# Sums of k and v and rows of o by head halves of the array, in a fused linear attention and softplus MLP

## The chip, the core and the metric

The kernel runs on one core of a Trainium2 chip. The metric is the device time of one execution in microseconds (us). Engines are named as the profile names them: PE is TensorE (matmul), PEld its weight loads, DVE is VectorE, ACT is ScalarE, POOL is GpSimd, SP is SyncE, which issues the DMA transfers here.

## What is computed

The reference is a linear attention without softmax, normed per head, followed by a two-layer MLP with a softplus between the layers.

```python
# q, k, v: (batch 8, heads 8, seq 576, head_dim 64), f32;  w_in: (512, 2048), w_out: (2048, 512)
kv  = np.einsum('bhsd,bhse->bhde', k, v)          # 64 x 64 per head
o   = np.einsum('bhsd,bhde->bhse', q, kv)
rms = np.sqrt(np.mean(o * o, axis=-1, keepdims=True) + 1e-06)
x   = (o / rms * g_norm)                          # then (B,H,S,D) -> (B*S, H*D) = (4608, 512)
h   = x @ w_in
g   = np.maximum(h, 0.0) + np.log1p(np.exp(-np.abs(h)))
out = g @ w_out
```

## The kernel before

The kernel is written as tasks. Each task names its engine, a planned duration in ns, what it has to wait for, the buffers that it takes and gives back, and a position. A planner in the program simulates the engines with these durations and fixes the order of the instructions on every engine; the chip then runs that order, with semaphores. `P0` is a list of 40 numbers that shift positions: when weights are fetched and converted, and how far ahead of the MLP the attention tiles and their transfers are put.

Tokens are treated in 36 tiles of 128. A batch has 576 tokens, 4.5 tiles, so four of the tiles are split between two batches (`parts(t)` then gives two parts of 64 rows). Three tiles make a block of 384 tokens for the MLP. The MLP, by far the most of the work, splits each f32 operand into three fp32r parts and runs at lines 668 (`h`) and 675 (`s`); the change does not touch it.

PSUM has eight banks: two for `h`, three for the sums `s0` to `s2` of the MLP, one for transposes `tp`, two in the ring `o`:

```python
rings = dict(m=13, xv=2, gv=2, g=2, raw=2, sq=1, ...,
             h=2, o=2, tp=1, s0=1, s1=1, s2=1)
kv_diag = [const.tile([P, NP, P], F32, name=f"kv_diag{i}") for i in range(2)]   # P=128, NP=4 pairs of heads
```

The sums of k and v for a batch. Head h and head h+4 make a pair p. Most batches lay a pair of heads of k side by side, so that one matmul on the whole array gives a 128 x 128 block, of which the two 64 x 64 blocks on the diagonal are wanted. Batches 0 and 1 (`wide_rows`) use a matmul per head, whose output takes half of the partitions:

```python
def kv_of(b):
    wide_rows = b < 2
    bank = slot("o")
    for p in range(NP + 1):                 # four steps of 512 rows in all, then a tail of 64 rows
        ...
            if s is ks and not wide_rows:   # k of batches 2 to 7: two DMAs
                for h in range(2):
                    nc.sync.dma_start(out=x[:, h::2], in_=src[:, h])
            else:
                nc.sync.dma_start(out=x.rearrange("s (h i) d -> s h i d", h=2), in_=src)
        ...
        def run(...):
            kv = new(bank, [P, NP, 2, D]) if p == 0 else bank.tile
            for i in range(4):
                if wide_rows and not tail:
                    for e in range(2):
                        l, r = (x.tile.rearrange("s (h i) d -> s h i d", h=2)[:, e, i] for x in (ks, vs))
                        nc.tensor.matmul(kv[e * D:(e + 1) * D, p, e], lhsT=l, rhs=r, ...)      # L505
                    continue
                if tail:
                    l, r = pairs(ks.tile, i), vs.tile[:, i::NP]
                else:
                    l, r = pairs(ks.tile, i), vs.tile.rearrange("s (h i) d -> s h i d", h=2)[:, :, i]
                nc.tensor.matmul(kv[:, i if tail else p], lhsT=l, rhs=r, ...)                  # L513
        last = add("PE", 1640 if wide_rows and not tail else 820, run, ...)
    kvd = kv_diag[b % 2]
    kv_ready[b] = [                          # the two diagonal blocks; the rest of kv_diag stays zero
        add("ACT", 360, lambda: nc.scalar.copy(kvd[:D, :, :D], bank.tile[:D, :, 0]), ...),
        add("ACT", 360, lambda: nc.scalar.copy(kvd[D:, :, D:], bank.tile[D:, :, 1]), ...)]
```

The rows of o for a tile. q comes transposed as `qT`, a pair of heads on the 128 partitions, and is multiplied by the pair's block-diagonal matrix. After that o is squared and summed (ACT, DVE), the root is taken (POOL), and o is scaled (DVE, `norm`):

```python
def rows(t):
    tp, qT, o, x, r, xp, xg = (slot(n) for n in ("tp", "m", f"s{t}" if t < TB else "o", "x", "r", "tp", "m"))
    def out_rows():
        y = new(o, [P, H, D])
        for b, r0, n, _ in parts(t):
            for p in range(NP):
                nc.tensor.matmul(y[r0:r0 + n, p::NP], lhsT=qT.tile[:, p, r0:r0 + n],           # L530
                                 rhs=kv_diag[b % 2][:, p].rearrange("r (h d) -> r h d", d=D), ...)
    ...
    a = o_task = add("PE", 830 if len(parts(t)) == 1 else 1350, out_rows, turned + need, pos, [o], [qT])
    a = add("ACT", 600, square of o into x, [a], pos, [x])
    a = add("DVE", 690, reduce, [a], pos, [r])
    a = add("POOL", 2300, root, [a], pos)
    a = add("DVE", 700, norm, [a, o_task], pos, [], [o, r])
```

(The line of the square is shortened here to what it does.) Until the MLP's first step, TensorE fills its idle time with matmuls that have no use but to keep it busy (L784).

Of the kernel before, what the change touches and what calls it, by code (L numbers as in the profile page):

```python
# [8 lines left out]
F32 = mybir.dt.float32  # L9
# [3 lines left out]
AF = mybir.ActivationFunctionType  # L13
ALU = mybir.AluOpType
# [4 lines left out]
P = 128  # L19
# [21 lines left out]
class Plan:  # L41
# [101 lines left out]
def kernel(  # L143
# [24 lines left out]
    nc = tc.nc  # L168
    B, H, S, D = q.shape
# [3 lines left out]
    NP = H // 2  # L173
    KD, KF = d_model // P, d_ff // P
    NT = 384
    TB = NT // P
# [6 lines left out]
    PLACES = 8  # L183
    LAST = PHASES[-1]

    P0 = [-71.0, -4.7, -70.3, -8.7, -15.1, -0.5, -23.9, 2.7, -65.0, -28.3, -35.2, -10.7, -25.2, 1.3,
          -0.2, -2.7, 0.5, -17.5, 13.0, 9.5, 5.5, 6.5, -2.0, 2.5, 2.5, 28.0, 15.0, 14.5, 8.5, 44.5,
          49.5, 68.5, 52.5, 72.0, 94.5, 99.5, 115.5, 110.5, 114.5, 8.5]
    CONVERT, FETCH, EARLY, LATER = P0[:8], P0[8:16], P0[16:27], P0[27:]
    BY_PE = 12  # L190
    AT_ONCE = 2 * TB
# [2 lines left out]
    const = ctx.enter_context(tc.tile_pool(name="const", bufs=1))  # L194
    sb = ctx.enter_context(tc.tile_pool(name="sb", bufs=1))
    ps = ctx.enter_context(tc.tile_pool(name="ps", bufs=1, space=PSUM))
    dram = ctx.enter_context(tc.tile_pool(name="dram", bufs=1, space=DRAM))

    ident_r = const.tile([P, P], F32R, name="ident_r")
# [6 lines left out]
    tails = [const.tile([P, H, D], F32, name=f"tail{i}") for i in range(2)]  # L206
    over = const.tile([P, 2 * KF], F32, name="over")
    scale = const.tile([P, 1], F32, name="scale")
    kv_diag = [const.tile([P, NP, P], F32, name=f"kv_diag{i}") for i in range(2)]


    rings = dict(m=13, xv=2, gv=2, g=2, raw=2, sq=1, 
                 tail0=1, tail1=1, qa=1, xb=1, x=2, r=2,
                 h=2, o=2, tp=1, s0=1, s1=1, s2=1)
    rings.update({f"w{i}_{c}": 1 for i in range(2) for c in range(PLACES)})
    PS = {"h", "o", "tp", "s0", "s1", "s2"}
    plan = Plan(rings)
    slot, add = plan.slot, plan.add

    def new(s, shape, dtype=F32):  # L220
        pool = ps if s.ring in PS else sb
        s.tile = pool.tile(shape, dtype, tag=f"{s.ring}_{s.place}", name=f"{s.ring}_{s.place}")
        return s.tile

    def pairs(x, p):

        return x[:, 2 * p:2 * p + 2].rearrange("r h d -> r (h d)")


    def halves(src, e):  # L230

        return src[e * NP:(e + 1) * NP].rearrange("p s d -> s p d")
# [155 lines left out]
    def parts(t):  # L388

        b, s0 = divmod(t * P, S)  # L390
        if s0 + P <= S:
            return [(b, 0, P, s0)]
        return [(b, 0, S - s0, s0), (b + 1, S - s0, P - S + s0, 0)]
# [63 lines left out]
    kv_ready = {}  # L457
    o_tasks = {}

    def x_pos(t):  # L460

        n = t // TB
        return t * EARLY[0] + EARLY[1] if n == 0 else first_step[0, n] - (EARLY[2] if n == 1 else EARLY[3]) + t % TB

    def kv_of(b):

        pos = x_pos(first_tile[b]) - (EARLY[4] if b else EARLY[5])
        wide_rows = b < 2
        bank = slot("o")
        last = None  # L470
        MAIN = 4 * P
        for p in range(NP + 1):
            tail = p == NP
            ks, vs = (slot(f"tail{i}" if tail else "m") for i in range(2))
            n = S - MAIN if tail else P

            def load(src, s, p=p, tail=tail, n=n, ks=ks):
                if tail:
                    s.tile = tails[s is not ks]
                    src = src[b, :, MAIN:]  # L480
                    if s is ks:
                        for e in range(2):
                            nc.sync.dma_start(out=s.tile[:n, e::2], in_=halves(src, e))
                    else:
                        nc.sync.dma_start(out=s.tile[:n], in_=src.rearrange("h s d -> s h d"))
                    return
                x = new(s, [P, H, D])
                src = src[b, p::NP, :MAIN].rearrange("h (s i) d -> s h i d", i=4)
                if s is ks and not wide_rows:
                    for h in range(2):  # L490
                        nc.sync.dma_start(out=x[:, h::2], in_=src[:, h])
                else:
                    nc.sync.dma_start(out=x.rearrange("s (h i) d -> s h i d", h=2), in_=src)

            lds = [add("SP", ns, lambda src=src, s=s, load=load: load(src, s), (), pos - EARLY[6] + 0.5 * p, [s], [],
                       620 if tail else size, behind=int(pos - 2) - 3)
                   for src, s, ns, size in ((k, ks, *((500, 850) if wide_rows and not tail else (900, 1300))), (v, vs, 500, 850))]

            def run(ks=ks, vs=vs, p=p, tail=tail, n=n):
                kv = new(bank, [P, NP, 2, D]) if p == 0 else bank.tile  # L500
                for i in range(4):
                    if wide_rows and not tail:
                        for e in range(2):
                            l, r = (x.tile.rearrange("s (h i) d -> s h i d", h=2)[:, e, i] for x in (ks, vs))
                            nc.tensor.matmul(kv[e * D:(e + 1) * D, p, e], lhsT=l, rhs=r, start=(p == 0 and i == 0),  # L505
                                             stop=False, skip_group_check=True)
                        continue
                    if tail:
                        l, r = pairs(ks.tile, i), vs.tile[:, i::NP]
                    else:  # L510
                        l, r = pairs(ks.tile, i), vs.tile.rearrange("s (h i) d -> s h i d", h=2)[:, :, i]

                    nc.tensor.matmul(kv[:, i if tail else p], lhsT=l, rhs=r, start=(p == 0 and i == 0), stop=tail,  # L513
                                     skip_group_check=True)
            last = add("PE", 1640 if wide_rows and not tail else 820, run, lds + [last], pos + 0.5 * p,
                       [bank] if p == 0 else [], [ks, vs])
        kvd = kv_diag[b % 2]
        old = o_tasks.get(b - 2, [])
        kv_ready[b] = [
            add("ACT", 360, lambda: nc.scalar.copy(kvd[:D, :, :D], bank.tile[:D, :, 0]), [last] + old, pos + 2.5, [], [bank]),  # L520
            add("ACT", 360, lambda: nc.scalar.copy(kvd[D:, :, D:], bank.tile[D:, :, 1]), [last] + old, pos + 2.5, [], [bank])]

    def rows(t):
        pos = x_pos(t)
        tp, qT, o, x, r, xp, xg = (slot(n) for n in ("tp", "m", f"s{t}" if t < TB else "o", "x", "r", "tp", "m"))
        def out_rows():
            y = new(o, [P, H, D])
            for b, r0, n, _ in parts(t):
                for p in range(NP):
                    nc.tensor.matmul(y[r0:r0 + n, p::NP], lhsT=qT.tile[:, p, r0:r0 + n],  # L530
                                     rhs=kv_diag[b % 2][:, p].rearrange("r (h d) -> r h d", d=D),
                                     start=(p == 0), stop=True, skip_group_check=True)

        def reduce():
            nc.vector.tensor_reduce(out=new(r, [P, H]), in_=x.tile, axis=AX.X, op=ALU.add)  # L535
# [3 lines left out]
            nc.gpsimd.tensor_tensor(out=r.tile, in0=r.tile, in1=half, op=ALU.pow)  # L539

        def norm():
            nc.vector.tensor_tensor(out=x.tile, in0=o.tile, in1=r.tile.unsqueeze(2).to_broadcast([P, H, D]), op=ALU.mult)  # L542

        def turn_x():
            y = new(xp, [P, KD, P])
# [8 lines left out]
        turned = []  # L554
        for b, r0, n, s0 in parts(t):
            if b >= 2:
                if b not in q_slots:
# [3 lines left out]
                        out=part_of_qT(n, r0),  # L561
                        in_=q_slots[b].tile.rearrange("k (p s) -> k p s", p=NP)[:, :, s0:s0 + n]),
# [24 lines left out]
            tp = turn_q.__defaults__[-1]  # L587
# [4 lines left out]
            turned.append(add("ACT", 590, lambda n=n, r0=r0, tp=tp: nc.scalar.copy(part_of_qT(n, r0), tp.tile[:, :, :n]),  # L592
                              [a], pos - 1, [qT] if not r0 else [], [tp], follows=turned[-1] if turned else None))
        need = [u for pt in parts(t) for u in kv_ready[pt[0]]]
        a = o_task = add("PE", 830 if len(parts(t)) == 1 else 1350, out_rows, turned + need, pos, [o], [qT])
        for pt in parts(t):
            o_tasks.setdefault(pt[0], []).append(a)
        a = add("ACT", 600, lambda: nc.scalar.activation(new(x, [P, H, D]), o.tile, func=AF.Square,  # L598
                                                              scale=D ** -0.5), [a], pos, [x])
        a = add("DVE", 690, reduce, [a], pos, [r])  # L600
        a = add("POOL", 2300, root, [a], pos)
# [146 lines left out]
        nc.scalar.dma_start(out=g_col[e * D:(e + 1) * D], in_=g_norm.rearrange("(d one) -> d one", one=1))  # L748
    nc.scalar.mul(g_down, g_col, DOWN_G)
    nc.scalar.preload_act_table_set("softplus")  # L750
    scratch = kv_diag[0][:, 0]
    make_identity(nc, scratch)
    nc.vector.tensor_copy(ident_r, scratch)
    nc.scalar.mul(minus_r, ident, -1.0)
    nc.vector.memset(half, -0.5)
    nc.vector.memset(big, 2.0 ** 30)
    for x in kv_diag + tails:
        nc.vector.memset(x, 0.0)

    for c in range(KF):  # L760
# [59 lines left out]
```

## Time and profile before

| | |
|---|---|
| time, median of 3 runs | 917.99 us (917.92 to 919.47) |
| span of the profiled execution | 917.5 us |
| granted TensorE clock | 1.00 |
| HBM read, written | 91.75 MB, 38.80 MB |
| DMA packets | 230,386, of which 127,408 under 512 B |
| k of batches 2 to 7 | 48 issues of 128 KB, median 4.1 us from issue to landing |
| v | 32 issues of 256 KB, median 4.2 us |

The page gives busy time by engine, then the span in 40 slices of about 23 us with the busy share of each in tenths, then the chain of work that ended last, then groups of instructions. A matmul on f32 operands leaves two weight loads and two matmul records. The ends of matmul records are modelled, so that sums of busy time of short groups on PE are longer than what the group occupies; the starts are read better. The attention lies at the beginning: the rows of o run from 23.3 to 319.6 us, the sums of k and v from 9.4 to 271.6 us, and the MLP's first matmul starts at 42.66 us.

### The profile page before, as it was taken

How to read it: one execution, taken by the hardware profiler on the slowest of the kernel's cores; microseconds unless marked ns; L12 is line 12 of the kernel's file. 1: busy time of each engine (PE TensorE's matmuls, PEld its weight loads, DVE VectorE, ACT ScalarE, POOL GpSimd, SP SyncE). 2: the span in 40 equal slices, each digit the busy share in tenths (PEclk: the TensorE clock that was granted, in tenths of full speed). 3: DMA queues.
4: the chain of work that ended last, by engine and by line, in shares of the span. 5: the costliest groups of instructions: out<-in, count | busy, mean ns of one | idle time of the engine just before them, and what ended most of it. 6: DMA issues, size and time to landing. Idle time of an engine off the chain costs nothing.

```text
span 917.5 us, 13377 instructions
## 1 busy us (share of the span) xinstructions
PE 898.1 (98%) x4863; PEld 812.4 (89%) x4863; DVE 626.6 (68%) x1055; ACT 415.1 (45%) x799; POOL 81.2 (9%) x78
## 2 busy tenths in 40 slices
PE   5799999999999999999999999999999999999998
PEld 4689999989998999999999999999999999998987
DVE  5877887875457887789856778888444455555553
ACT  4776555444334656455434455446323333333331
POOL 0324421312122100000000000000000000000000
PEclk9999999999999999999999999999999999999999
DMA  7999999397883654445433434643320433333323
GB/s 226 241 224 224 260 207 203 89 216 147 176 139 108 149 150 127 125 139 172 149 104 127 150 126 139 208 142 122 104 70 33 138 102 103 106 104 104 104 69 104
DMA packets 230386, 131.44 MB, mean 143 GB/s; under 512 B 127408, under 2 KB 204208, under 8 KB 230320
## 3 DMA queue, kind: packets, MB, share of 16 engines
q1 hardware_dynamic: 230160, 130.59, 53.7%
q8 instruction: 38, 0.62, 0.3%
q14 instruction: 28, 0.23, 0.1%
q10 hardware_dynamic: 160, 0.00, 0.0%
HBM read 91.75 MB, written 38.80 MB: 142 GB/s over the span
## 4 chain that ended last, share of the span: by engine, by line
PE 95%; DMA 2%; DVE 1%; ACT 1%; SPq 0%; issue 0%; ACTq 0%
PE s L675 44%; PE h L668 43%; PE o L530 3%; PE o L513 3%; DMA m<-in_v_dram 1%; DMA g_col<-in_g_norm_dram 1%; PE tp L547 0%; DMA tail<-in_k_dram 0%; SPq L608 0%; PE o L505 0%; PE h L367 0%; DVE xv L440 0%; DVE xv L444 0%; PE tp L585 0%; ACT L750 0%
## 5 line engine op out<-in xcount | busy, mean ns | idle before, releaser
L668 PE MATMUL h<-xv,w 128*128 128x384 f32 x2304 | 434.3, 337 | 0.9 <-ACT g L688 0.9
L675 PE MATMUL s<-w,gv 128*128 128x512 f32 x1728 | 434.2, 395 | 0.0
L668 PEld LDWEIGHTS h<-xv,w 128*128 128x128 f32 x2304 | 406.6, 188 | 15.9 <-ACT g L688 1.1
L675 PEld LDWEIGHTS s<-w,gv 128*128 128x128 f32 x1728 | 319.4, 188 | 58.9 <-issue 0.5
L688 ACT ACTIVATE g<-h 128x384 f32<-128x384 f32 x192 | 94.3, 491 | 392.7 <-PE h L668 388.2
L679 DVE TENSOR_TENSOR gv<-g,gv 128x384 fp32r<-128x384 f32 x192 | 106.4, 554 | 179.1 <-ACT gv L690 178.2
L690 ACT ACTIVATE gv<-g 128x384 fp32r<-128x384 f32 x192 | 100.9, 525 | 22.9 <-PE s L675 15.6
L683 DVE SCALAR_TENSOR_TENSOR gv<-gv 128x384 fp32r<-128x384 f32 x192 | 106.9, 557 | 6.1
L440 DVE SCALAR_TENSOR_TENSOR xv<-m,g_col,xv 128x512 fp32r<-128x512 f32 x102 | 75.9, 744 | 1.3 <-ACT xv L437 1.1
L444 DVE SCALAR_TENSOR_TENSOR xv<-xv 128x512 fp32r<-128x512 f32 x108 | 74.4, 689 | 2.6
L437 ACT ACTIVATE xv<-m,g_down 128x512 fp32r<-128x512 f32 x102 | 69.5, 710 | 1.1 <-DMA m<-x 1.1
L539 POOL TENSOR_TENSOR r<-r,half 128x8 f32<-128x8 f32 x36 | 65.5, 1818 | 3.0
L715 DVE SCALAR_TENSOR_TENSOR m<-s,scale,m 128x512 f32<-128x512 f32 x24 | 17.9, 747 | 30.1 <-PE s L675 30.1
L530 PE MATMUL o<-kv_diag,m 128*128 128x128 f32 (+1 forms) x296 | 36.9, 275 | 0.0
L530 PEld LDWEIGHTS o<-kv_diag,m 128*128 128x128 f32 (+1 forms) x296 | 35.1, 179 | 2.0 <-issue 1.0
L538 POOL TENSOR_SCALAR r<-r 128x8 f32<-128x8 f32 x36 | 15.1, 419 | 240.9 <-DVE r L535 240.6
L715 DVE SCALAR_TENSOR_TENSOR m<-s,m 128x512 f32<-128x512 f32 x36 | 23.7, 684 | 13.5 <-PE s L675 13.4
L542 DVE TENSOR_TENSOR x<-o,r 128x512 f32<-128x512 f32 x33 | 22.7, 687 | 13.5 <-POOL r L539 13.4
L535 DVE TENSOR_REDUCE r<-x 128x8 f32<-128x512 f32 x36 | 24.5, 680 | 10.2 <-ACT x L598 10.0
L303 ACT ACTIVATE sq<-sq,big 128x512 bf16<-128x512 bf16 x32 | 22.9, 717 | 11.2 <-DVE m L299 11.1
L286 ACT ACTIVATE sq<-raw 128x512 bf16<-128x512 bf16 x32 | 21.2, 664 | 12.5 <-DMA raw<-in_moe_w_in_dram 8.3
L299 DVE SCALAR_TENSOR_TENSOR m<-sq,m 128x512 f32<-128x512 bf16 x32 | 22.1, 690 | 6.3 <-ACT sq L286 4.9
(69 smaller groups left out, 452.8 us busy)
## 6 DMA issues: line engine op xcount, KB each, us to landing
m<-x SPq DMA_DIRECT2D x102, 256.0 KB, 4.7
part<-m SPq DMA_DIRECT2D x72, 256.0 KB, 2.7
m<-part SPq DMA_DIRECT2D x72, 256.0 KB, 3.7
raw<-in_moe_w_in_dram SPq DMA_DIRECT2D x16, 512.0 KB, 5.7
m<-in_v_dram SPq DMA_DIRECT2D x32, 256.0 KB, 4.2
raw<-in_moe_w_out_dram SPq DMA_DIRECT2D x16, 512.0 KB, 5.1
qa<-in_q_dram SPq DMA_DIRECT2D x24, 288.0 KB, 6.3
m<-in_k_dram SPq DMA_DIRECT2D x48, 128.0 KB, 4.1
```

Of the source, the lines that this page charges most:

```text
L437: nc.scalar.activation(cols(0, F32R), x.tile, func=AF.Identity, scale=g_down)
L440: nc.vector.scalar_tensor_tensor(out=cols(1, F32R), in0=x.tile, scalar=g_col, in1=cols(0), op0=ALU.mult, op1=ALU.subtract)
L444: nc.vector.scalar_tensor_tensor(out=cols(2, F32R), in0=cols(1), scalar=-RADIX, in1=cols(0), op0=ALU.mult, op1=ALU.add)
L530: nc.tensor.matmul(y[r0:r0 + n, p::NP], lhsT=qT.tile[:, p, r0:r0 + n], rhs=kv_diag[b % 2][:, p].rearrange("r (h d) -> r h d", d=D), start= ...
L539: nc.gpsimd.tensor_tensor(out=r.tile, in0=r.tile, in1=half, op=ALU.pow)
L668: nc.tensor.matmul(hp, lhsT=w_in.tile[:, i, kd * P:(kd + 1) * P], rhs=xv.tile[:, i, kd], start=(m == 0), stop=(m == 3 * KD - 1))
L675: nc.tensor.matmul(mine[i].tile, lhsT=gv.tile[:, m, i * P:(i + 1) * P], rhs=w_out.tile[:, m], start=(c == cs[0] and m == 0), stop=(c == cs ...
L679: nc.vector.tensor_tensor(out=gv.tile[:, 1], in0=g.tile, in1=gv.tile.bitcast(F32)[:, 0], op=ALU.subtract)
L683: nc.vector.scalar_tensor_tensor(out=gv.tile[:, 2], in0=f32[:, 1], scalar=-RADIX, in1=f32[:, 0], op0=ALU.mult, op1=ALU.add)
L688: a = add("ACT", 490, lambda: nc.scalar.activation(new(g, [P, NT]), h.tile, func=AF.Softplus, scale=1.0 + E), [a], s, [g], [h])
L690: a = add("ACT", 530, lambda: nc.scalar.activation(new(gv, [P, 3, NT], F32R)[:, 0], g.tile, func=AF.Copy, scale=DOWN), [a], s, [gv])
L715: a = add("DVE", 700, lambda: nc.vector.scalar_tensor_tensor(out=new(ot, [P, d_model]), in0=bank.tile, scalar=(scale if ph == LAST else 1. ...
```

## The change

The sums of k and v are formed a head at a time for all batches: the head's 64 columns of k are the weights, and its output takes one half of the partitions, so two heads use the two column halves of the array. The block-diagonal matrix goes away; `kv` holds for each pair one head in the upper and one in the lower 64 partitions, and is copied out in one instruction. The rows of o are also formed a head at a time: a head's 64 rows of qT and its 64 x 64 matrix use one row half of the array. The outputs of the two row halves go to two different banks. A tile's o is then half of each of two banks, and the two places of the ring `o` are the two halves of the same pair of banks. The sums of k and v no longer use `o`: batches 0 and 1 use `s0` and `s1`, the others `tp`. All of k is loaded in one DMA per step, in runs of four rows of a head (1 KB), as v is. The planned durations and the positions `P0` are set anew. The aim is to let the two halves of the array work at the same time on f32 matmuls that before computed zeros, or blocks that nobody needs.

```diff
-    P0 = [-71.0, -4.7, -70.3, -8.7, -15.1, -0.5, -23.9, 2.7, -65.0, -28.3, -35.2, ...]
+    P0 = [-76.5, -1.2, -72.8, -8.7, -7.1, 2.0, -30.9, 0.7, -53.5, -44.8, -49.2, ...]
+    o_banks = ps.tile([P, 2, 2, NP, D], F32, name="o_banks")
-    kv_diag = [const.tile([P, NP, P], F32, name=f"kv_diag{i}") for i in range(2)]
+    kvs = [const.tile([P, NP, D], F32, name=f"kv{i}") for i in range(2)]
-    PS = {"h", "o", "tp", "s0", "s1", "s2"}
+    PS = {"h", "tp", "s0", "s1", "s2"}
 ... kv_of
-        wide_rows = b < 2
-        bank = slot("o")
+        bank = slot(f"s{b}" if b < 2 else "tp")
 ...
-                if s is ks and not wide_rows:
-                    for h in range(2):
-                        nc.sync.dma_start(out=x[:, h::2], in_=src[:, h])
-                else:
-                    nc.sync.dma_start(out=x.rearrange("s (h i) d -> s h i d", h=2), in_=src)
+                nc.sync.dma_start(out=new(s, [P, 2, 4, D]), in_=src[b, p::NP, :MAIN].rearrange("h (s i) d -> s h i d", i=4))
 ...
+                    for e in range(2):
+                        l, r = (x.tile[:, i + e * NP] if tail else x.tile[:, e, i] for x in (ks, vs))
+                        nc.tensor.matmul(kv[e * D:(e + 1) * D, i if tail else p], lhsT=l, rhs=r,
+                                         start=(p == 0 and i == 0), stop=tail, skip_group_check=True)
-            last = add("PE", 1640 if wide_rows and not tail else 820, run, ...)
+            last = add("PE", 450, run, lds + [last], pos + 0.5 * p, [bank] if p == 0 else [], [ks, vs])
+        kv_ready[b] = [add("ACT", 400, lambda: nc.scalar.copy(kvs[b % 2], bank.tile), ...)]
 ... rows
-        tp, qT, o, x, r, xp, xg = (slot(n) for n in ("tp", "m", f"s{t}" if t < TB else "o", "x", "r", "tp", "m"))
+        tp, qT, o, x, r, xp, xg = (slot(n) for n in ("tp", "m", "o", "x", "r", "tp", "m"))
 ...
-                    nc.tensor.matmul(y[r0:r0 + n, p::NP], lhsT=qT.tile[:, p, r0:r0 + n],
-                                     rhs=kv_diag[b % 2][:, p].rearrange("r (h d) -> r h d", d=D),
-                                     start=(p == 0), stop=True, skip_group_check=True)
+                    for e in range(2):
+                        nc.tensor.matmul(o_of()[r0:r0 + n, e, p], lhsT=qT.tile[e * D:(e + 1) * D, p, r0:r0 + n],
+                                         rhs=kvs[b % 2][e * D:(e + 1) * D, p], start=True, stop=True)
+        def o_of():
+            return o_banks[:, :, o.place]
 ...
-        a = o_task = add("PE", 830 if len(parts(t)) == 1 else 1350, out_rows, turned + need, pos, [o], [qT])
+        a = o_task = add("PE", 500, out_rows, turned + need, pos, [o], [qT])
 ... at the start: one tile fewer kind to clear
-    for x in kv_diag + tails:
+    for x in tails:
         nc.vector.memset(x, 0.0)
```

More of the change, by code (lines that the diff above doesn't have):

```diff
@@ L184 @@
     LAST = PHASES[-1]
-    P0 = [-71.0, -4.7, -70.3, -8.7, -15.1, -0.5, -23.9, 2.7, -65.0, -28.3, -35.2, -10.7, -25.2, 1.3,
-          -0.2, -2.7, 0.5, -17.5, 13.0, 9.5, 5.5, 6.5, -2.0, 2.5, 2.5, 28.0, 15.0, 14.5, 8.5, 44.5,
-          49.5, 68.5, 52.5, 72.0, 94.5, 99.5, 115.5, 110.5, 114.5, 8.5]
+    P0 = [-76.5, -1.2, -72.8, -8.7, -7.1, 2.0, -30.9, 0.7, -53.5, -44.8, -49.2, -10.7, -28.2, 0.8, -0.2,
+          -3.7, 0.5, -17.0, 13.0, 9.5, 5.5, 6.0, -2.0, 2.5, 3.5, 32.5, -5.5, 14.5, 8.5, 41.5, 47.5,
+          68.0, 54.5, 73.5, 89.5, 95.5, 115.5, 110.5, 114.0, 8.5]
     CONVERT, FETCH, EARLY, LATER = P0[:8], P0[8:16], P0[16:27], P0[27:]
@@ L479, in load @@
                     s.tile = tails[s is not ks]
[L480 to L483, printed above, removed]
-                    else:
-                        nc.sync.dma_start(out=s.tile[:n], in_=src.rearrange("h s d -> s h d"))
-                    return
-                x = new(s, [P, H, D])
-                src = src[b, p::NP, :MAIN].rearrange("h (s i) d -> s h i d", i=4)
@@ L489, in load @@
-                if s is ks and not wide_rows:
-                    for h in range(2):
-                        nc.sync.dma_start(out=x[:, h::2], in_=src[:, h])
-                else:
-                    nc.sync.dma_start(out=x.rearrange("s (h i) d -> s h i d", h=2), in_=src)
-            lds = [add("SP", ns, lambda src=src, s=s, load=load: load(src, s), (), pos - EARLY[6] + 0.5 * p, [s], [],
-                       620 if tail else size, behind=int(pos - 2) - 3)
-                   for src, s, ns, size in ((k, ks, *((500, 850) if wide_rows and not tail else (900, 1300))), (v, vs, 500, 850))]
@@ L499, in run @@
-            def run(ks=ks, vs=vs, p=p, tail=tail, n=n):
-                kv = new(bank, [P, NP, 2, D]) if p == 0 else bank.tile
-                for i in range(4):
[L502 to L521, printed above, removed]
+                    nc.sync.dma_start(out=s.tile[:n], in_=src[b, :, MAIN:].rearrange("h s d -> s h d"))
@@ new lines, in load, with run @@
+                    return
+                nc.sync.dma_start(out=new(s, [P, 2, 4, D]), in_=src[b, p::NP, :MAIN].rearrange("h (s i) d -> s h i d", i=4))
+            lds = [add("SP", 500, lambda src=src, s=s, load=load: load(src, s), (), pos - EARLY[6] + 0.5 * p, [s], [],
+                       650 if tail else 850, behind=int(pos - 2) - 3) for src, s in ((k, ks), (v, vs))]
+            def run(ks=ks, vs=vs, p=p, tail=tail):
+                kv = new(bank, [P, NP, D]) if p == 0 else bank.tile
+                for i in range(4):
+                    for e in range(2):
+                        l, r = (x.tile[:, i + e * NP] if tail else x.tile[:, e, i] for x in (ks, vs))
+                        nc.tensor.matmul(kv[e * D:(e + 1) * D, i if tail else p], lhsT=l, rhs=r,
+                                         start=(p == 0 and i == 0), stop=tail, skip_group_check=True)
@@ L523, in rows, with heads @@
+            last = add("PE", 450, run, lds + [last], pos + 0.5 * p, [bank] if p == 0 else [], [ks, vs])
+        kv_ready[b] = [add("ACT", 400, lambda: nc.scalar.copy(kvs[b % 2], bank.tile), [last] + o_tasks.get(b - 2, []),
+                           pos + 2.5, [], [bank])]
+    def heads(x):
+        return x.rearrange("s (e p) d -> s e p d", e=2)
     def rows(t):
         pos = x_pos(t)
-        tp, qT, o, x, r, xp, xg = (slot(n) for n in ("tp", "m", f"s{t}" if t < TB else "o", "x", "r", "tp", "m"))
+        tp, qT, o, x, r, xp, xg = (slot(n) for n in ("tp", "m", "o", "x", "r", "tp", "m"))
@@ L526, in out_rows @@
         def out_rows():
-            y = new(o, [P, H, D])
             for b, r0, n, _ in parts(t):
                 for p in range(NP):
-                    nc.tensor.matmul(y[r0:r0 + n, p::NP], lhsT=qT.tile[:, p, r0:r0 + n],
-                                     rhs=kv_diag[b % 2][:, p].rearrange("r (h d) -> r h d", d=D),
-                                     start=(p == 0), stop=True, skip_group_check=True)
+                    for e in range(2):
+                        nc.tensor.matmul(o_of()[r0:r0 + n, e, p], lhsT=qT.tile[e * D:(e + 1) * D, p, r0:r0 + n],
+                                         rhs=kvs[b % 2][e * D:(e + 1) * D, p], start=True, stop=True)
@@ L541, in norm @@
         def norm():
-            nc.vector.tensor_tensor(out=x.tile, in0=o.tile, in1=r.tile.unsqueeze(2).to_broadcast([P, H, D]), op=ALU.mult)
+            nc.vector.tensor_tensor(out=heads(x.tile), in0=o_of(), in1=r.tile.rearrange("s (e p) -> s e p", e=2).unsqueeze(
+                3).to_broadcast([P, 2, NP, D]), op=ALU.mult)
         def turn_x():
@@ L594, in rows @@
         need = [u for pt in parts(t) for u in kv_ready[pt[0]]]
-        a = o_task = add("PE", 830 if len(parts(t)) == 1 else 1350, out_rows, turned + need, pos, [o], [qT])
+        a = o_task = add("PE", 500, out_rows, turned + need, pos, [o], [qT])
         for pt in parts(t):
             o_tasks.setdefault(pt[0], []).append(a)
-        a = add("ACT", 600, lambda: nc.scalar.activation(new(x, [P, H, D]), o.tile, func=AF.Square,
+        a = add("ACT", 600, lambda: nc.scalar.activation(heads(new(x, [P, H, D])), o_of(), func=AF.Square,
                                                               scale=D ** -0.5), [a], pos, [x])
@@ L750 @@
     nc.scalar.preload_act_table_set("softplus")
-    scratch = kv_diag[0][:, 0]
+    scratch = kvs[0].rearrange("r p d -> r (p d)")[:, :P]
     make_identity(nc, scratch)
```

## The prediction

> **What bounds the kernel now.** I read the busy shares and slices of the page first, then the chain, the groups by shape, and last the order of single instructions on TensorE.
>
> ```profile
> PE 898.1 (98%) x4863; PEld 812.4 (89%) x4863; DVE 626.6 (68%) x1055; ACT 415.1 (45%) x799; POOL 81.2 (9%) x78
> ...
> PE   5799999999999999999999999999999999999998
> PEclk9999999999999999999999999999999999999999
> DMA  7999999397883654445433434643320433333323
> ...
> PE s L675 44%; PE h L668 43%; PE o L530 3%; PE o L513 3%; DMA m<-in_v_dram 1%; DMA g_col<-in_g_norm_dram 1%; PE tp L547 0%; DMA tail<-in_k_dram 0%; SPq L608 0%; PE o L505 0%; PE h L367 0%; DVE xv L440 0%; DVE xv L444 0%; PE tp L585 0%; ACT L750 0%
> ```
>
> From the third slice (46 us) to the end TensorE has no hole, at full clock, and the chain is 95% PE. So an instruction taken off TensorE after about 40 us shortens the run by what it occupied, until something else becomes the bound. Before 40 us it does not: by the windows PE is busy 26.8 of those 40 us, 7.4 of them with the filler matmuls of L784, while the DMA share is 0.86.
>
> The change touches the sums of k and v (L505, L513) and the rows of o (L530). By shape:
>
> ```profile
> L530 PE MATMUL o<-kv_diag,m 128*128 128x128 f32 x232 | 30.5, 274 | 0.0
> L513 PE MATMUL o<-m,m 128*128 128x128 f32 x192 | 24.9, 275 | 0.7 <-DMA m<-in_v_dram 0.7
> ...
> L513 PE MATMUL o<-tail,tail 128*128 128x128 f32 x64 | 8.9, 283 | 0.0
> ...
> L505 PE MATMUL o<-m,m 128*64 128x64 f32 x128 | 7.0, 272 | 6.8 <-DMA m<-in_v_dram 6.8
> ...
> L530 PE MATMUL o<-kv_diag,m 128*64 128x128 f32 x64 | 6.3, 279 | 0.0
> ```
>
> One matmul call on f32 leaves two records (96 calls of L513 with m are x192), so four calls, one group, are 8 records. The busy sums contain modelled ends (8 records read 1.05 us), so I take starts from the order of time:
>
> ```profile
> 65.00 0.97 PEld L530 LDWEIGHTS o<-kv_diag,m 128*128 128x128 f32 x8
> 65.11 1.06 PE L530 MATMUL o<-kv_diag,m 128*128 128x128 f32 x8
> ...
> 65.90 0.19 PEld L366 LDWEIGHTS h<-w,ident_r 128*128 128x128 f32 x1
> ```
>
> The weight loads of the group begin at 65.00 and those of the next task at 65.90: a full-array group occupies **0.90 us**, and the single records start 112 ns apart. The same holds for L513. This is the unit that must shrink.
>
> The kernel before already has one piece in the new form: the sums of batches 0 and 1 at L505, one head on each column half.
>
> ```profile
> 30.64 0.69 PE L505 MATMUL o<-m,m 128*64 128x64 f32 x16 [1.40 <-DMA m<-in_v_dram]
> 31.26 0.66 PE L547 MATMUL tp<-ident_r,x 128*128 128x128 f32 x4
> ```
>
> Here 16 records start between 30.64 and 31.10, 29 to 31 ns apart on average, though each half streams its own record in about 58 ns: two halves at once. They occupy 0.47 us; the next task starts 0.15 us after the last record.
>
> **What the Trainium skill says.** (1) TensorE: Matmul & The Clock Gate, section LDWEIGHTS (loading the stationary operand): a load takes its columns over 1.2 per ns, whatever the number of rows. The trace agrees: loads of 128 columns read 192 ns and of 64 columns 138 ns, 54 ns for 64 columns; and around L741, whose matmul has one column only, successive 128-column loads start 108 ns apart (632.915, 633.023). (2) TensorEngine Tiling (Array Packing), Key Properties: different tiles can load and multiply in parallel, and changing the tiling drains the engine. L505 shows the first for column halves. For the second: from an L675 matmul to a half-array one takes 0.327 us against 0.231 to the next L675 one; from L668 0.268 against 0.174; out of the split rows of L530 0.202 against 0.109. Each switch costs **0.095 us**. (3) Same page, Gotcha 1: PSUM Pressure: row tiles may not write one bank at the same time. That is why the two halves of o get two banks; no run here shows it yet. (4) PSUM — Partial Sum Buffer, PSUM bank collisions raise a hardware error: two engines may not be in one bank and quadrant at once. In the change both places of o lie in the same two banks, so accesses to one place must be kept apart from those to the other. The trace before, with a bank per place, cannot show what that costs.
>
> **Part 1: sums of k and v.** By the windows 16 of L513's 256 records come before 40 us, so 240 records, 30 groups, lie on the saturated engine. Each goes from 0.90 to 0.47 us of records plus at most two switches, 0.47 + 0.19 = 0.66: 0.24 saved when alone, 0.33 where a neighbour uses the same tiling and a switch falls away. At 0.27 this is 30 x 0.27 = **8 us saved**. L505 itself keeps its form.
>
> **Part 2: rows of o.** 36 tiles, four of them split between two batches. 32 of 320 records come before 40 us; after it are 28 full groups and all 4 split tiles. Now lhsT has 64 rows and still 128 columns, against 64 moving columns. The matmul part of a record halves to some 54 ns, but its weight load is still 128 columns, about 110 ns. Everything hangs on what row halves do with their loads:
> - A: the loads cost no more than in L505. A group is 0.47 + 0.19 = 0.66, saving 0.24; 28 x 0.24 = 6.7 us.
> - B: the two halves load in parallel but each needs its 110 ns: 8 x 0.112 + 0.19 = 1.09, a loss of 0.19; 28 x 0.19 = 5.3 us lost.
> - C: the loads queue: 16 x 0.107 + 0.19 = 1.90, a loss of 1.0; 28 us lost.
>
> Split tiles now occupy 1.51 us and a switch in, 1.60. Afterwards loads and streams both have 64 columns: 32 records at 29 ns plus 0.19 = 1.12, saving 0.5 x 4 = 2 us in each case.
>
> **Part 3: transfers.** For batches 2 to 7 k comes now as two 128 KB issues in 256-byte runs: 6 x 8 x 512 = 24,576 runs become 6,144, 18,432 fewer of 230,160 packets of the queue (8%). PE waited for a v transfer after 40 us only 0.7 us in all, so this is headroom: the windows give a DMA share of 1.00 and 1.06 at 40 to 120 us, where a shorter TensorE schedule would otherwise run into DMA. Together with the re-tuned positions and two memsets fewer at the start I allow 2.5 us gained, a guess.
>
> **Part 4: copies and banks.** Two ACT copies of 64 partitions (353 ns each) become one of about 400; ACT is not the bound. The kv sums move to the s banks and to tp, which has one place. The shared banks of o order the square and the norm of one tile against the rows of the next; the norm is some 4 us behind its rows (square 0.6, reduce 0.68, POOL 2.2, norm 0.69), and 36 tiles pass in about 290 us, so mostly they miss each other. I allow 1 us of new PE waits.
>
> **Sums.** A: -8 - 6.7 - 2 - 2.5 + 1 = -18, 900 us. B: -8 + 5.3 - 2 - 2.5 + 1 = -6, **912 us**. C: -8 + 28 - 2 - 2.5 + 1 = +16, 934 us.
>
> **The rivals.** Case B is what the two load figures say, as the number of rows does not shorten a load. For A speaks the change itself: its plan books 500 ns for a group of rows (830 before) and 450 for a group of sums (820 before), and the earlier bookings match the trace within a tenth (0.90, and 0.43 for transposes booked at 440). Somebody may have measured 500. Against it: 500 is also booked for split tiles, booked at 1350 before, so it may be no measurement. C contradicts the page on tiling and would have made the booking wrong by a factor of four. A further rival: PE waits at the shared banks of o or at tp, several us when square or norm runs late, with DVE busy 78 to 82% in 40 to 160 us. It would add 5 to 10 us to any case. Last, DMA could hold the shortened stretch at 40 to 120 us and take back some of part 1; the wider runs of k speak against that.
>
> **Range and chances.** I give A 0.32, B 0.60, C 0.08. The weighted mean is 0.32 x 900 + 0.60 x 912 + 0.08 x 934 = 910; as the plan's positions have been tuned again for this form, I set 908. Faster by over 2% means under 899.6: half of A and a little of B, 0.22. Slower by over 2% means over 936.4: half of C and a little for waits, 0.05. Range 894 to 922, from a good A to a B with waits.
>
> **What would show it.** Right for part 1: the sums all have 128*64 records, 16 in a group, starts 29 to 31 ns apart, 0.095 us more at both ends. For part 2 the spacing of the 64*128 records of the rows decides: about 30 ns on average is A, 55 is B, 107 is C. Waits of PE on ACT or DVE by name of o_banks or tp, or idle PE slices between 40 and 320 us, would show the bank rival. Packets should fall by about 18,000. I am wrong if the rows are spaced as in A and the time still stays above 905, or if the gain comes from before 40 us, where I book almost nothing.

## Result and profile after

The changed kernel takes 924.93 us (median of 4 runs, 923.5 to 927.33) against 918.03 us (917.92 to 919.47): a ratio of 1.0074, 95% interval 1.005 to 1.0099. It is slower by 6.9 us; the prediction had a gain of 10.

The page of the changed kernel, in the order of the lines shown before:

```profile
PE 907.5 (98%) x5457; PEld 802.3 (87%) x5457; DVE 624.4 (68%) x1053; ACT 413.3 (45%) x791; POOL 79.5 (9%) x78
...
PE   7989999999999999999999999999999999999998
...
DMA packets 211447, 131.52 MB, mean 143 GB/s; under 512 B 102320, under 2 KB 185264, under 8 KB 211376
...
PE s L660 44%; PE h L653 43%; PE o_banks L512 4%; PE tp L495 2%; DMA g_col<-in_g_norm_dram 1%; PE tp L532 1%; PE h L769 0%; PE tp L570 0%; DMA m<-in_q_dram 0%; DVE r L519 0%; DVE xv L441 0%; DVE x L526 0%; POOL r L523 0%; ACT m L592 0%; PE s L495 0%
```

PE still ends the run. The chain is 4% rows and 2% sums where it was 3% and 3%; and the third slice, about 46 to 69 us, shows an 8 where the kernel before has a 9. Packets fell by 18,939; 18,432 had been worked out.

The groups by shape on PE (line, tile of the array, shape and count, then busy us and mean ns):

```profile
L512 PE MATMUL o_banks<-kv,m 64*128 64x64 f32 x512 | 35.5, 278 | 0.4 <-DVE x L526 0.3
L769 PE MATMUL h<-ident_r 128*128 128x512 f32 x39 | 17.4, 554 | 1.7 <-DVE ident_r L738 1.6
L495 PE MATMUL tp<-m,m 128*64 128x64 f32 x384 | 16.0, 228 | 0.0
...
L512 PE MATMUL o_banks<-kv,m 64*64 64x64 f32 x128 | 3.9, 224 | 0.3 <-DVE x L526 0.3
```

The last line is the four split tiles. Filler (L769) rose from 21 matmuls to 39. In order of time, groups of rows and of sums in the kernel before (the view ends inside the last group):

```profile
86.44 1.06 PE L530 MATMUL o<-kv_diag,m 128*128 128x128 f32 x8
87.26 0.94 PE L675 MATMUL s<-w,gv 128*128 128x512 f32 x3
88.04 1.05 PE L513 MATMUL o<-m,m 128*128 128x128 f32 x8
88.85 0.94 PE L675 MATMUL s<-w,gv 128*128 128x512 f32 x3
89.63 0.61 PE L513 MATMUL o<-tail,tail 128*128 128x128 f32 x4
```

and in the changed kernel:

```profile
88.67 1.11 PE L512 MATMUL o_banks<-kv,m 64*128 64x64 f32 x16
89.71 1.65 PE L660 MATMUL s<-w,gv 128*128 128x512 f32 x6
91.30 0.69 PE L495 MATMUL tp<-m,m 128*64 128x64 f32 x16
91.91 0.96 PE L660 MATMUL s<-w,gv 128*128 128x512 f32 x3
92.80 0.69 PE L495 MATMUL tp<-tail,tail 128*64 128x64 f32 x16
```

From the start of a rows group to the next task are 1.04 us, from that of a sums group 0.61. Over all neighbours of one kind, records of rows (64*128) start 55.8 ns apart on average, records of sums (128*64) 32.5 ns, and records of the split tiles (64*64) 24 ns. So the sums are spaced about as L505 had shown, and the rows as in case B.

The cost of a whole group is another matter. A sums group and the three `s` matmuls behind it take 1.50 us (91.30 to 92.80) where they took 1.59 (88.04 to 89.63): 0.09 us saved, and not 0.24 to 0.33. A rows group and six `s` matmuls take 2.63 us (88.67 to 91.30); without three of them, at 0.231 each, that is 1.94, against 1.60 before (86.44 to 88.04): 0.34 lost, and not 0.19. The single starts around the sums group at 91.30 show where it goes: 0.09 us more than usual before the first record, 0.46 from the first record to the last, 0.15 from there to the next task, and 0.10 more than usual between that task's first two matmuls, about 0.8 in all. Groups that stand alone between MLP matmuls take 0.80 to 0.82 us for sums and 1.23 us or more for rows, against 0.89 on the whole array.

Case B gave 912 us by the prediction's sum, not 925. The group cost is one part of what is missing. A new hole is another. The stretch behind the sums of batch 2, all engines:

```profile
57.03 0.69 PE L495 MATMUL tp<-m,m 128*64 128x64 f32 x16
...
62.06 0.64 PE L495 MATMUL tp<-tail,tail 128*64 128x64 f32 x16
...
62.74 0.37 ACT L498 COPY kv<-tp 128x256 f32<-128x256 f32 x1 [2.18 <-PE tp L495]
...
63.17 0.66 PE L532 MATMUL tp<-ident_r,x 128*128 128x128 f32 x4 [0.47 <-ACT kv L498]
...
63.86 0.69 ACT L438 ACTIVATE xv<-tp,g_down 128x512 fp32r<-128x512 f32 x1 [0.21 <-PE tp L532]
...
65.06 0.75 DVE L441 SCALAR_TENSOR_TENSOR xv<-tp,g_col,xv 128x512 fp32r<-128x512 f32 x1 [0.69 <-ACT m L592]
...
65.87 1.12 PE L570 MATMUL tp<-ident_r,m 128*128 128x128 f32 x4 [2.04 <-DVE xv L441]
...
66.64 0.78 PE L367 MATMUL h<-w,ident_r 128*128 128x512 f32 x1
```

The sums of batch 2 hold the bank tp from 57.03 us to the end of their copy at 63.1. Transposes that need tp line up behind them, and each must be read out by ACT and DVE before the next may write: PE waits 0.47 us, then 2.04 us. After the hole the matmuls run slowly (a group of four transposes 1.12 us instead of 0.60 to 0.66); the windows give a granted clock of 0.66 over these 5 us, and of 0.50 from 66 to 68 us (columns: stretch, busy us of PE, PEld, DVE, ACT, POOL, then PEclk):

```profile
65.00:70.00 5.00, 4.13 (x27) 3.19 (x28) 3.81 (x6) 2.47 (x6) 0.00 (x0) 0.66 0.85 132
```

Also the first MLP matmul starts at 43.97 us instead of 42.66.

### The profile page after: what moved, and what is told of

It is laid out like the page before. It is cut to its first block, busy times and chain, and to the rows that moved or that the text cites. A ratio compares the mean times of both kernels' runs of the same rounds, so it can differ in the third digit from the quotient of the medians.

```text
span 922.5 us, 14514 instructions
## 1 busy us (share of the span) xinstructions
PE 907.5 (98%) x5457; PEld 802.3 (87%) x5457; DVE 624.4 (68%) x1053; ACT 413.3 (45%) x791; POOL 79.5 (9%) x78
## 4 chain that ended last, share of the span: by engine, by line
PE 95%; DVE 2%; ACT 1%; DMA 1%; issue 0%; POOL 0%; ACTq 0%; SPq 0%; DVEq 0%
PE s L660 44%; PE h L653 43%; PE o_banks L512 4%; PE tp L495 2%; DMA g_col<-in_g_norm_dram 1%; PE tp L532 1%; PE h L769 0%; PE tp L570 0%; DMA m<-in_q_dram 0%; DVE r L519 0%; DVE xv L441 0%; DVE x L526 0%; POOL r L523 0%; ACT m L592 0%; PE s L495 0%
## 5 line engine op out<-in xcount | busy, mean ns | idle before, releaser
L523 POOL TENSOR_TENSOR r<-r,half 128x8 f32<-128x8 f32 x36 | 63.2, 1755 | 3.0
L512 PEld LDWEIGHTS o_banks<-kv,m 64*128 64x128 f32 (+1 forms) x640 | 34.4, 176 | 10.0 <-issue 6.4
L512 PE MATMUL o_banks<-kv,m 64*128 64x64 f32 (+1 forms) x640 | 39.3, 267 | 0.8 <-DVE x L526 0.7
L526 DVE TENSOR_TENSOR x<-o_banks,r 128x512 f32<-128x512 f32 x36 | 24.7, 686 | 20.2 <-PE o_banks L512 9.8
L583 ACT ACTIVATE x<-o_banks 128x512 f32<-128x512 f32 x36 | 21.4, 599 | 21.2 <-PE o_banks L512 17.1
L352 DVE TENSOR_TENSOR m<-m,w 128x512 f32<-128x512 f32 x30 | 20.5, 685 | 9.5 <-ACT w L349 9.5
```

The costliest lines, as they stand in the source:

```text
L512: nc.tensor.matmul(o_of()[r0:r0 + n, e, p], lhsT=qT.tile[e * D:(e + 1) * D, p, r0:r0 + n], rhs=kvs[b % 2][e * D:(e + 1) * D, p], start=Tru ...
```

## Experiments

Each was timed in five rounds beside the kernel before, which read 917.9 to 918.4 us. A run's ratio and interval are against that kernel. The median of the changed kernel is itself known to about 2.3 us either way, so differences to it of 1 or 2 us are not clear of noise.

**1. Sums in halves, alone, in the old order.** From the kernel before:

```diff
-                if s is ks and not wide_rows:        # k in two DMAs
+                if s is ks and not halves_too:       # halves_too = True
-                    if wide_rows and not tail:
+                    if halves_too and not tail:
```

> The kernel before, in which all batches form their sums a head at a time on column halves and load k in 1 KB runs; tails and rows stay on the whole array, and the planned durations, so the order of instructions, stay untouched. Theory one (the halves of the sums pay, those of the rows do not): 24 groups after 43 us shrink by 0.18 to 0.24 us each, 4.3 to 5.8 us, so 912 to 914. Theory two (the switches of tiling eat the gain of the sums too): 917 to 919. Theory three (the loss lies in the new order alone): the sums gain here as theory one says, so this run parts two from the others.

Measured: 916.06 us, ratio 0.9977 (0.997 to 0.9984). A gain, but of 1.9 us and not 4 to 6: theory two, the cost of the switches, has most of the truth. At 0.09 us a group, as read above, the 24 groups give about 2.

**2. Rows back on the whole array, in the order of the change** (block-diagonal matrix, two copies by ACT, one bank a place, planned durations untouched):

```diff
-   nc.tensor.matmul(o_of()[r0:r0 + n, e, p], lhsT=qT.tile[e * D:(e + 1) * D, p, r0:r0 + n], rhs=kvs[b % 2][e * D:(e + 1) * D, p], ...)
+   nc.tensor.matmul(y[r0:r0 + n, p::NP], lhsT=qT.tile[:, p, r0:r0 + n], rhs=kv_diag[b % 2][:, p]..., ...)
```

> The changed kernel with its order of instructions untouched, but with the rows of o back on the whole array (a pair at a time with the block-diagonal matrix, a bank for each place of o). Theory one: each of some 28 whole groups becomes 0.13 us shorter, the four split tiles some 0.4 us longer, so 2 to 3 us less than the changed kernel, 922 to 923. Theory three (order alone): no difference beyond 1 us, 924 to 926. Were the shared banks of o a cost on TensorE, it would fall by more than 4 us.

Measured: 919.78 us, ratio 1.0017 (1.0008 to 1.0026), 5.1 us under the changed kernel. The row halves cost more than the expectation had. The sign set for the shared banks, over 4 us, was passed, but in the changed kernel's trace PE waits only 0.7 us in all on o_banks.

**3. Sums back on the whole array, in the order of the change**, with k in two transfers and two copies by ACT:

```diff
-                    for e in range(2):   # kv[e * D:(e + 1) * D, ...], a head at a time
+                    nc.tensor.matmul(kv[:, i if tail else p], lhsT=pairs(...), rhs=..., ...)
```

> The changed kernel with its order of instructions untouched, but with the sums as before (whole array but for the steps of batches 0 and 1, k in two transfers of 256-byte runs); the rows stay on row halves. Theory one: 30 groups become 0.2 us longer, 930 to 932. Theory two (sums in halves do not pay): 924 to 926 or less. Theory three: 930 to 932 as well, for the sums are then innocent.

Measured: 930.89 us, ratio 1.0142 (1.0128 to 1.0156): 6.0 us worse, as theories one and three had it. The sums in halves, with their loads of k, are worth 6 us in this order; part of that is a longer spell of half clock, 68.7 to 75.6 us against 65.3 to 68.7 in the changed kernel.

**4. The changed kernel with the old positions**, `P0` alone put back.

> The changed kernel with the list of positions P0 of the kernel before, nothing else. Theory three (the loss lies in the new order): 915 to 919. Theory one with the instructions to blame: within 2 us of the changed kernel, 923 to 927. If transposes still wait at the single bank of tp while the sums of batch 2 sit in it, PE idle of 2 to 3 us near 60 us stays as it is.

Measured: 930.01 us, ratio 1.013 (1.0117 to 1.0144). Both expectations missed: the new positions save the changed kernel 5.1 us. They are not its fault. The idle of 2.3 us at tp is there with the old ones too.

**5. All sums in halves, tails too, in the old order** (as 1, with `if halves_too:` and the tail of k in one DMA).

> As the earlier run with sums in halves in the order of the kernel before, and now the tails too (all 40 groups of the sums on column halves, all of k in its natural layout); rows on the whole array, order untouched. Theory one: 6 more groups after 43 us at 0.15 to 0.24 us, and six pairs of switches that fall away where a tail follows a step: 1 to 2 us under 916.1, so 914 to 915. If the tails gain nothing: 916.

Measured: 915.13 us, ratio 0.9963 (0.9951 to 0.9976). The lowest of all (12 and 18 are level with it), and it beats both kernels. The sums of batch 2 in this trace sit in a bank of o, and the transposes in tp run between them, without a wait:

```profile
57.85 0.69 PE L503 MATMUL o<-m,m 128*64 128x64 f32 x16
58.47 0.66 PE L583 MATMUL tp<-ident_r,m 128*128 128x128 f32 x4
59.05 0.69 PE L503 MATMUL o<-m,m 128*64 128x64 f32 x16
59.80 0.66 PE L583 MATMUL tp<-ident_r,m 128*128 128x128 f32 x4
60.39 0.69 PE L503 MATMUL o<-tail,tail 128*64 128x64 f32 x16
```

**6. Rows in 64 x 64 tiles**: the changed kernel with twice as many row matmuls, of 64 tokens each, which shortens the weight loads to 64 columns and uses four tiles of the array in place of two.

```diff
-            for b, r0, n, _ in parts(t):
+            for b, r0, n in [(b, r, 64) for b, r0, n, _ in parts(t) for r in range(r0, r0 + n, 64)]:
```

> The changed kernel, order untouched, in which each row matmul of 128 tokens is cut into two of 64 tokens: twice as many instructions, 64 x 64 tiles, weight loads of 64 columns. Theory one (rows are bound by the 128-column loads): a group becomes 32 records at 24 to 28 ns instead of 16 at 56, 0.1 us shorter, 28 whole groups: 2 to 4 us less, 921 to 923. If the streaming of the 64 moving columns or the count of instructions bounds the rows instead, the time rises by up to 0.9 us a group, to 940 or more.

Measured: 921.06 us, ratio 1.0033 (1.002 to 1.0045), 3.9 us less. The group with twice the instructions is the shorter one:

```profile
54.10 0.97 PE L512 MATMUL o_banks<-kv,m 64*64 64x64 f32 x32
55.01 2.37 PE L660 MATMUL s<-w,gv 128*128 128x512 f32 x9
```

0.91 us for 32 records against 1.04 for 16. The moving side is 64 columns in both, so neither streaming nor the count of instructions bounds the rows. In the changed kernel each row half starts a record every 112 ns, near the 108 ns at which 128-column loads follow each other at L741: the loads are the likely bound. The run does not part shorter loads from four tiles working at once.

**7. As 2, with the sums in the ring o** (`bank = slot("o")`); the planner finds another order.

> The changed kernel with rows on the whole array, as run before at 919.8, but the sums of k and v accumulate in the ring o, as in the kernel before, and no longer in tp and s. Its planner finds another order, the positions P0 are those of the change. Theory four (the single bank of tp, shared by sums and transposes, costs 3 to 4 us near 62 to 68 us): 915 to 917 and no idle stretch of PE over 1 us after 45 us. If tp is innocent: 919 to 921.

Measured: 920.94 us, ratio 1.0029 (1.0019 to 1.0039). That is the number of an innocent tp. The hole at 62 to 68 us is gone, but a wait at tp of 0.8 us, before 61.5 us, and others elsewhere have come, for instance 1.0 us before 185.86 for ACT, and the MLP starts at 45.58 us. So taking the sums out of tp does not by itself win the loss back.

**8. The kernel before with the new positions.**

> The kernel before with the list of positions P0 of the change, nothing else. If the new positions were good in themselves it would be at or under 918; if they are fitted to the other form, as the old ones proved to be for the changed kernel (5 us), 920 to 925.

Measured: 918.56 us, ratio 1.0003 (0.9994 to 1.0011): neutral, between the two expectations.

**9. Transposes of tiles 5 to 7 in h**, out of the way of the sums in tp:

```diff
-        tp, qT, o, x, r, xp, xg = (slot(n) for n in ("tp", "m", "o", "x", "r", "tp", "m"))
+        tp, qT, o, x, r, xp, xg = (slot(n) for n in ("tp", "m", "o", "x", "r", "h" if 5 <= t < 8 else "tp", "m"))
```

> The changed kernel, in which the transposes of x of tiles 5 to 7 go to a bank of h instead of tp; up to the sums of batch 2 the order on TensorE stays. Theory four (tp is held by the sums of batch 2 and the transposes pile up behind it): the idle 2 us at 64 to 66 us and the slow matmuls after it go, the MLP is 3 to 4 us further at 80 us, and the time is 921 to 922. If the tp stall only moves or h becomes the stall instead: 924 to 926.

Measured: 923.32 us, ratio 1.0054 (1.0042 to 1.0066), 1.6 us less than the changed kernel, between the two expectations and not clear of noise. No wait over 0.5 us is left between 43 and 90 us, and from the first MLP matmul to 15 us of MLP work (matmuls of `h` and `s` at 174 and 231 ns) it takes 30.4 us against 33.4. But its MLP started at 45.69 us, with the same order on TensorE up to there as the changed kernel's 43.97: that start varies between executions. The clock was at half for 10.2 us of this start (9.9 to 13.3 and 16.7 to 23.5 us), and for 3.4 us of the other (17.5 to 20.9).

**10. Less filler**: the filler booked at 700 ns in the changed kernel, 20 of them instead of 39.

> The changed kernel with the filler matmul booked at 700 ns instead of 400, so that the planner inserts fewer of them before the MLP. Theory five (the shorter bookings of the sums made room for 18 more fillers, which take longer than booked and delay the start): the first MLP matmul at 42.5 to 43 us instead of 44.0, the time 1 to 1.5 us less, 923.4 to 924. If the filler is innocent: 924 to 926, or more where the clock drops.

Measured: 926.66 us (923.55 to 929.22), ratio 1.0085 (1.0068 to 1.0102). In the profiled execution the MLP starts at 42.90 us as theory five had it, the hole at tp stays (longest wait 2.0 us), and the median gains nothing.

**11. As 5, all sums booked at 500 ns** instead of 1640 and 820, k booked like v.

> All sums in halves in the kernel before (915.1 with the old bookings), now booked at 500 ns a group, near what they take, and the loads of k as those of v. Theory six (bookings near the truth give a better order): 912 to 914. Theory five (short bookings bring filler and a later start): the first MLP matmul 1 to 3 us later and 916 to 918.

Measured: 918.47 us, ratio 0.9999 (0.999 to 1.0008), 3.3 us worse than 5, with 36 fillers and a first MLP matmul at 45.01 us. Between 43 and 100 us PE idles 2.6 us against 0.1 in 5, most of it a wait of 1.6 us for a copy of the sums.

**12. As 5, with the new positions.**

> All sums in halves in the kernel before, old bookings, with the list P0 of the change. P0 alone moved the kernel before by 0.6 us at most. If it is neutral here too: 914.5 to 916.5; if it suits halves in general: 912 to 914.

Measured: 915.48 us, ratio 0.9967 (0.9954 to 0.998): neutral again. Its MLP starts at 44.75 us, 2 us later than in 5, so a late start by itself is not a loss.

**13. The changed kernel with only the first sums booked long:**

```diff
-            last = add("PE", 450, run, ...)
+            last = add("PE", (1640 if not tail else 820) if b < 2 else 450, run, ...)
```

> The changed kernel, in which only the sums of batches 0 and 1 are booked as long as before (1640 ns a step, 820 the tail), so that the planner leaves the start as dense in filler as before or less. Theory five b (the short bookings at the start, not the filler's own, delay the MLP and let the clock fall): the first MLP matmul at 42.5 to 43.5 us with a clock of 1.0 in the first slices, and 2 to 3 us less than the changed kernel, 922 to 923. If bookings at the start are innocent: 924 to 927.

Measured: 926.81 us, ratio 1.009 (1.0077 to 1.0103). The MLP starts at 41.92 us, earlier than in any other run here, and nothing is gained. PE waits longer at tp, and the clock is at half for 6.8 us (62.3 to 69.1) against 3.4. The waits of PE from 43 to 90 us (waiting, releaser: us in total, times, longest):

```profile
PE tp L532 <- ACT kv L498: 2.4, 1, 2.4
PE tp L570 <- DVE xv L441: 1.0, 1, 1.0
```

**14. As 13, with transposes of tiles 5 to 7 in h.**

> As the run before, with the transposes of tiles 5 to 7 in h besides. If the late start and the stall at tp are separate costs that add: 1.6 to 3 us less than the run before, 919 to 921. If they are one and the same: no more than either alone.

Measured: 925.55 us, ratio 1.0084 (1.0067 to 1.0101). A miss: 1.3 us, which is not clear of noise, and 5 us off the 920 of a sum.

**15. As 14, with the rows on the whole array.**

> As the run before, with the rows of o on the whole array besides. If start, stall and row halves are the three losses and add: 5 us less than the run before, 914 to 916, as good as all sums in halves in the kernel before (915.1). If something else of the change still costs: 917 to 920.

Measured: 919.44 us, ratio 1.0011 (1.0003 to 1.002). The rows give 6.1 us, about as in 2; the rest does not come back.

**16. The banks of the change alone, put into 5:**

```diff
-        bank = slot("o")
+        bank = slot(f"s{b}" if b < 2 else "tp")
-        ... = (slot(n) for n in ("tp", "m", f"s{t}" if t < TB else "o", "x", "r", "tp", "m"))
+        ... = (slot(n) for n in ("tp", "m", "o", "x", "r", "tp", "m"))
```

> All sums in halves in the kernel before (915.1), rows on the whole array, old positions and bookings, with the banks of the change alone: the sums of batches 0 and 1 in s0 and s1, the others in tp, and the rows of all tiles in o. Theory four b (the move of the sums to the single bank of tp is what costs the rest of the loss): 919 to 923, with idle PE at 55 to 70 us. If the banks are innocent in themselves: 914 to 917, and the loss lies in how positions and bookings were set.

Measured: 918.79 us, ratio 1.0002 (0.9994 to 1.0011), 3.7 us worse than 5 and just under what theory four b had. PE has one wait of 1.9 us at tp, near 67 us.

**17. Only the sums of batches 2 to 7 moved to tp**, `bank = slot("o" if b < 2 else "tp")` in 5.

> As the run before, but the sums of batches 0 and 1 and the first rows keep their old banks; only those of batches 2 to 7 sit in tp. Theory four b: 918 to 922, most of the same loss. If the banks of the first sums and rows matter instead: 914 to 917.

Measured: 923.48 us, ratio 1.0063 (1.0051 to 1.0076), 8.4 us worse than 5, by one expression in the program and the order that the planner then chose. That is beyond what was expected, and more than all the banks together cost in 16. Where 5 has no wait of PE that the view lists between 43 and 90 us, this run has

```profile
PE tp L583 <- DVE xv L440: 2.0, 1, 2.0
PE tp L545 <- DVE xv L440: 1.5, 1, 1.5
```

and in order of time, behind the sums that end at 60.5 us, the mark of the changed kernel:

```profile
63.16 0.60 PE L545 MATMUL tp<-ident_r,x 128*128 128x128 f32 x4
...
66.30 0.66 PE L545 MATMUL tp<-ident_r,x 128*128 128x128 f32 x4 [1.47 <-DVE xv L440]
69.00 1.11 PE L583 MATMUL tp<-ident_r,m 128*128 128x128 f32 x4 [2.04 <-DVE xv L440]
```

Between 43 and 100 us PE idles 3.9 us here, 2.5 in 16 and 0.1 in 5. Half clock, from 68.0 to 74.8 us, costs 3.4 us here; 16 keeps its clock (1.00 from 60 to 80 us), and so does 5. Idle time and clock together are 7.1 of the 8.4 us.

**18. As 5, with only the later sums booked at 500 ns.**

> All sums in halves in the kernel before, with the sums of batches 2 to 7 booked at 500 ns and those of batches 0 and 1 as long as before. All booked at 500 gave 918.5, with the first MLP matmul 2.3 us later. If the bookings of the first sums were its loss: the start at 42.5 to 43 us and 913.5 to 915.5. If the loss came from the order of the later ones: 917 to 919.

Measured: 915.34 us, ratio 0.997 (0.996 to 0.998), MLP from 43.17 us. So the loss of 11 came from the bookings of the first sums, or from those of k, not from the later sums.

## Why the prediction failed, by its own steps

Three steps failed: the cost of a group in Parts 1 and 2, the gain in Part 3, and the bank `tp` in Part 4.

**The bound** was read rightly for the steady part and carried too far forward. "From the third slice (46 us) to the end TensorE has no hole" was true only roughly: the kernel before idles 1.5 us between 45 and 55 us. The changed one reached 10 us of MLP work at 60.99 us (before: 67.59), then had to wait, and reached 20 us of it at 87.65 (before: 84.40).

**Part 1** (8 us saved by the sums) had the spacing right and the cost of a group wrong. "0.47 + 0.19 = 0.66" leaves out the 0.15 us from the last record to the next task, which I had read from the trace myself. A group that stands alone measures 0.81, so it saves 0.08 to 0.09 us where I had 0.27: 2.3 to 2.7 us for 30 groups. In the old order the sums measured 2.8 (experiment 5), in the order of the change 6.0, half clock included (3).

**Part 2** has the same gap. The spacing is that of case B, 55.8 ns, but "8 x 0.112 + 0.19 = 1.09" also lacks the time to the next task: a group measures 1.24, against 0.89 before. I set the net loss at 3.3 us and it measured 5.1 (2). The Trainium skill, TensorE: Matmul & The Clock Gate, section LDWEIGHTS (loading the stationary operand), says that a load goes by its columns and that fewer rows do not shorten it; this trace agrees, with a record every 112 ns in each row half. The booking of 500 ns, for which I gave case A 0.32, is half of what the group takes.

**Part 3** counted the packets rightly, but its 2.5 us of gain were a guess, and no such gain shows. The positions save the changed kernel 5.1 us (4), but do nothing for the kernel before (8) or for the sums in halves (12). In the kernel with all sums in halves, short bookings cost 3.3 us (11 against 5).

**Part 4** says: "The kv sums move to the s banks and to tp, which has one place", and puts no cost on it beyond 1 us of waits in all. Moving the later sums to tp, alone, costs 8.4 us (17), and all the banks of the change 3.7 (16), each with the planner's new order. I had named waits at tp as a rival of 5 to 10 us, but left it out of the weighted mean. The shared banks of o, which I priced, cost PE 0.7 us of waits. What I had not thought of is the clock: in the changed kernel and in 17 half clock follows the hole, for 3.4 and 6.8 us, and costs half of that.

**The sum.** The traces split the loss by stages. From 40 to 320 us of MLP work (its matmuls counted at 174 and 231 ns) PE neither waits nor loses its clock in the kernel before, the changed one, or experiments 2, 5 and 6, so positions and waits drop out. This stretch has 20 groups of sums, 19 whole groups of rows and two split tiles. It takes 318.7 us before, 320.9 changed, 316.9 with the rows back on the whole array (2), 316.2 with all sums in halves alone (5) and 318.3 with rows in 64 x 64 tiles (6). Case B gave it 20 x 0.27 saved, 19 x 0.19 lost and 2 x 0.5 saved, 2.8 us of gain; it lost 2.2. So 5 us of the miss are the cost of the groups alone. Up to 40 us of MLP work the changed kernel is 2.6 us behind (115.5 against 112.9), where the prediction's terms for case B had it some 3 us ahead. Here PE idles 1.4 us more, and half clock costs 1.7. The profiled executions are 5.0 us apart and the medians 6.9.

What stays open is how the loss of the early stretch divides between tp, the bookings and the planner's answer to them. Experiments 13 to 15 show that removing one wait lets another grow, and 7 that taking the sums out of tp did not win it back; that the bank, with the order then planned, can cause a loss of this size is shown in 17.

## What to carry to other kernels

Price a short group by all the time that it takes from the full-array work on both sides of it, not by the spacing of its records and a cost per switch: here 0.47 us of records cost 0.81. Half-array tiles paid, a little, where the stationary side shrank as well as the moving side; with a stationary side of 128 columns and a moving side of 64 they lost, and cutting the stationary side in two was the faster form. Before a PSUM bank is given a second user, look at who else waits for it: an accumulation over several microseconds in a single bank blocks every short user, and they come back as a chain of write, read, write, which here was long enough to cost the clock as well. When a trace has one engine full, check that the other engines could feed it faster in that same stretch, before its savings are counted there.

## What the runs showed of the hardware

On f32, four 64 x 64 tiles together start a record every 24 ns, against 32.5 ns for two column halves and 55.8 ns for two row halves with 128-column loads. A group on column halves that stands alone between full-array matmuls takes 0.34 us beyond its 0.47 us of records.

TensorE's clock fell to half in a hole whose longest wait was 2.04 us: from 62.7 to 65.9 us the engine ran only four transposes, the granted clock was 0.50 from 66 to 68 us, and 1.00 again from 69. Experiment 16, with one wait of 1.9 us, kept it. The Trainium skill, TensorE: Matmul & The Clock Gate, Part 4: PE-mode transpose, says that transposes do not count as busy in the same way as other matmuls, and that full clock does not engage for them; that fits this stretch, though no run here tests it apart from the hole.
